# A gated mix of attention and feed-forward: the first head's query tile filled on chip, and new prices in VectorE's budget

## The chip, the core and the metric

One core of a Trainium2 chip runs one program. The time is the device time of an execution in microseconds. Engines: TensorE (PE; its weight loads are shown as PEld), VectorE (DVE), ScalarE (ACT), GpSimd (POOL), and SyncE (SP), which issues nearly all DMAs, in order.

## The reference

```python
q = (x @ wq) in 32 heads of 16;  k = x @ wk;  v = x @ wv      # one k and v for all heads
a = concat_h(softmax(q_h @ k.T * 16**-0.5) @ v) @ wo
b = (silu(x @ w_gate) * (x @ w_up)) @ w_down
g = sigmoid((x * gate_w).sum(-1))
out = g * a + (1 - g) * b       # x: 2048 x 512, w_gate: 512 x 1792, all float32
```

## The kernel before

The 2048 rows of x are four chunks `c` of 512. Products that need float32 accuracy are made of three matmuls of a high and a low part (names ending in h and l). The 512 query columns are four groups `m` of 8 heads; `query(m, c)` (L229) is one job of 12 matmuls into a PSUM tile `pf`, of which there are three.

When a query job is done, its `keep` (L242) makes three 128x512 tiles from `pf`: the high part, the low part, and a bound on the scores. For early jobs ScalarE does the high part and the bound (L257, L258) and VectorE the low part (L259) and a maximum (`most`, L276). Each tile's 16 rows per head then go to the DRAM tensor `q_d` (L265), four stores of 256 KB per job, one of them the high part again. A head `h` is later read back as one tile `qs` of 512 KB, from `q_d[h]` (L672 for head 0, L688 for the others).

**Opening.** x is transposed, k and v are projected, then the four jobs `query(0, c)` run, then (1,2), (1,3) and (2,3) in `fill(GAP)` (L675). Between them SP gets the stores, the load of the fourth query weight (L671), the load of head 0's `qs` (L672) and the loads of the first gate and up weight (L144). A loaded weight lies in one of two buffers `wraw` until POOL has split it into two parts (L111, L112).

**Main part.** 128 blocks follow, four per head. A block (L749) makes eight score tiles (L698, two matmuls each, into two PSUM buffers `pss`), for which ScalarE takes the exponential (L706), part of it from a copy by VectorE (L702). Between the scores, in an order written out in STEPS, stand 16 steps of other matmuls (L198): query jobs that are left, gate, up and down projections. Each of these jobs is done in two halves of 64 rows, and the second half follows a marker, a tiny memset on VectorE (L446). At the end stand the products of exponentials and values (L718), whose sum over a head is divided on VectorE (L727, L730).

**VectorE's budget.** Work that may wait is put in a list, DEFER, with a price: the gate's multiply after the tanh (`silu`, L321, 0.7), the cast of gate times up in two parts (L111, L112, 1.2), and for late query jobs `scale` (L269), `bound` (L272, and then the store of the bound) and `most` (L276). At the end of a block, BUDGET = 3.8 is what may be done (L781 to L797): first items of the division, then three passes over DEFER: items of gates from earlier blocks, items of a gate whose tanh was in this block (in the set FRESH), and query items. What does not fit stays. If a gate's multiply is still in the list when its up projection is done, the up step does it itself, just ahead of its own product (L330, L331).

## Time and profile before

| | us |
|---|---|
| median of 3 runs | 1348.66 |
| lowest, highest | 1347.03, 1348.97 |
| the profiled execution | 1348.94 |
| its span, first to last instruction | 1347.0 |
| PE, ACT, DVE, POOL busy in the span | 1328.4, 1076.9, 722.0, 221.4 |

A row of the timeline is: start, duration, engine, line, operation, written tile <- read tiles, shapes, count; in brackets the idle time of the engine ahead of it and what ended that. A row of waits is: who <- whom, total, times, longest. Rows with SPq are DMA issues.

### The profile page before, as it was taken

What the parts mean: (1) busy time and instruction counts of PE and PEld (TensorE: products, weight loads), DVE (VectorE), ACT (ScalarE), POOL (GpSimd) and SP (SyncE); (2) the same over time, 40 slices, a digit from 0 to 9 for tenths busy, and PEclk for the clock granted to TensorE, in tenths of its full rate; (3) what the DMA queues carried; (4) which work ended last, traced back from release to release, by engine and by line L of the source; (5) the groups of instructions that cost most, each with busy time, mean ns of one, the idle gap of its engine ahead of it and who ended that gap; (6) DMA issues with size and microseconds to landing.
All of it is one profiled execution on the core that took longest, in us unless ns stands there. A gap on an engine that the chain in (4) does not pass through costs nothing. (4 is left out here: it accounts for less than half of the span.)

```text
span 1347.0 us, 26709 instructions
## 1 busy us (share of the span) xinstructions
PE 1328.4 (99%) x10743; PEld 767.6 (57%) x10743; DVE 722.0 (54%) x1237; ACT 1076.9 (80%) x1508; POOL 221.4 (16%) x227
## 2 busy tenths in 40 slices
PE   9899999999999999999999999999999999999998
PEld 7655555555555555555555555555555555555586
DVE  5346664654655664565465565456455565455442
ACT  4488898888888888888888888888888888888511
POOL 6352211420321430232110000000000000001222
PEclk9799999999999999999999999999999999999999
DMA  8851211411351751462262442243132342233164
GB/s 279 275 160 41 75 37 43 122 44 36 102 190 58 257 155 35 153 208 83 68 198 104 123 152 83 68 129 96 40 114 64 118 156 68 99 107 114 40 196 143
DMA packets 101041, 156.03 MB, mean 116 GB/s; under 512 B 11568, under 2 KB 42544, under 8 KB 99248
## 3 DMA queue, kind: packets, MB, share of 16 engines
q1 hardware_dynamic: 99184, 154.05, 35.9%
q8 instruction: 88, 1.44, 0.5%
q10 hardware_dynamic: 1728, 0.20, 0.1%
q14 instruction: 41, 0.34, 0.1%
HBM read 98.63 MB, written 55.57 MB: 114 GB/s over the span
## 5 line engine op out<-in xcount | busy, mean ns | idle before, releaser
L706 ACT ACTIVATE pt<-pss 128x1024 f32<-128x1024 f32 (+1 forms) x1024 | 833.0, 864 | 172.8 <-PE pss L698 146.4
L702 DVE COPY pt<-pss 128x512 f32<-128x512 f32 x381 | 263.5, 692 | 449.9 <-PE pss L698 413.8
L718 PE MATMUL po<-pt,vaug 128*32 128x512 f32 x4096 | 466.0, 595 | 0.0
L698 PE MATMUL pss<-qs,ks 64*128 64x512 f32 x2048 | 400.4, 416 | 6.7 <-DMA qs<-q_d 4.5
L698 PEld LDWEIGHTS pss<-qs,ks 64*128 64x128 f32 x2048 | 192.0, 185 | 219.5 <-ACT pt L706 172.3
L718 PEld LDWEIGHTS po<-pt,vaug 128*32 128x32 f32 x4096 | 120.0, 109 | 263.5 <-issue 257.8
L706 ACT ACTIVATE pt<-pt 128x512 f32<-128x512 f32 x381 | 210.5, 620 | 0.0
L198 PE MATMUL pf<-xh,wgh 64*128 64x512 f32 (+1 forms) x440 | 163.3, 392 | 2.2 <-DVE sign L446 1.8
L198 PE MATMUL pf<-xh,wgl 64*128 64x512 f32 (+1 forms) x440 | 162.7, 391 | 0.0
L198 PE MATMUL pf<-xl,wgh 64*128 64x512 f32 (+1 forms) x440 | 162.6, 391 | 0.0
L198 PE MATMUL pf<-xh,wuh 64*128 64x512 f32 (+1 forms) x440 | 161.0, 392 | 0.1
L198 PE MATMUL pf<-xh,wul 64*128 64x512 f32 (+1 forms) x440 | 160.2, 392 | 0.0
L198 PE MATMUL pf<-xl,wuh 64*128 64x512 f32 (+1 forms) x440 | 159.5, 390 | 0.0
L198 PE MATMUL pf<-wdh,hl 64*128 64x512 f32 (+1 forms) x427 | 143.5, 390 | 0.0
L198 PE MATMUL pf<-wdh,hh 64*128 64x512 f32 (+1 forms) x427 | 143.1, 392 | 0.0
L198 PE MATMUL pf<-wdl,hh 64*128 64x512 f32 (+1 forms) x427 | 142.8, 390 | 0.0
L727 DVE RECIPROCAL rsb<-rsb 128x128 f32<-128x128 f32 x128 | 117.0, 935 | 7.1 <-issue 4.5
L474 POOL CAST xh<-wraw 128x512 fp32r<-128x512 f32 x4 | 2.4, 611 | 548.2 <-DMA wraw<-o_d 548.2
L198 PEld LDWEIGHTS pf<-xh,wgh 64*128 64x128 f32 (+1 forms) x440 | 79.5, 185 | 12.5 <-issue 3.3
L198 PEld LDWEIGHTS pf<-xh,wuh 64*128 64x128 f32 (+1 forms) x440 | 78.7, 185 | 9.9 <-issue 1.7
L198 PEld LDWEIGHTS pf<-xl,wgh 64*128 64x128 f32 (+1 forms) x440 | 79.8, 185 | 5.7
L198 PEld LDWEIGHTS pf<-xh,wgl 64*128 64x128 f32 (+1 forms) x440 | 79.8, 185 | 5.6
(136 smaller groups left out, 1368.0 us busy)
## 6 DMA issues: line engine op xcount, KB each, us to landing
qs<-q_d SPq DMA_DIRECT2D x32, 512.0 KB, 4.9
wraw<-in_B_w_gate_dram SPq DMA_DIRECT2D x28, 256.0 KB, 3.5
wraw<-in_B_w_up_dram SPq DMA_DIRECT2D x28, 256.0 KB, 3.7
wraw<-in_B_w_down_dram SPq DMA_DIRECT2D x28, 256.0 KB, 4.0
wgh<-w_d SPq DMA_DIRECT2D x28, 256.0 KB, 2.8
wgl<-w_d SPq DMA_DIRECT2D x28, 256.0 KB, 3.0
wuh<-w_d SPq DMA_DIRECT2D x28, 256.0 KB, 2.7
wul<-w_d SPq DMA_DIRECT2D x28, 256.0 KB, 2.9
```

Source lines behind the costliest of these rows:

```text
L198: ins = nc.tensor.matmul(self.ps, a, b, start=(i == 0 and not half), stop=(last and half != 0))
L474: nc.gpsimd.tensor_copy(OT[c][0][:, k, :], raw)
L698: nc.tensor.matmul(ps[:, b * CH:(b + 1) * CH], ks[rows, kt * P:(kt + 1) * P], QS[h][rows, j, :], start=True, stop=True)
L702: other = nc.vector.tensor_copy(pt[:, CH:], ps[:, CH:]) if half else None
L706: ins = nc.scalar.activation(pt[:, w], ps[:, w], AF.Exp, scale=SCALE)
L718: nc.tensor.matmul(po[c * 2 * DH:(c + 1) * 2 * DH, :], vaug[:, kt, :], pt[:, c * CH:(c + 1) * CH], start=(kt == 0), stop=(kt == NT - 1))
L727: nc.vector.reciprocal(rsb[:, w], rsb[:, w])
```

## The change

Three edits.

1. Head 0's `qs` is no longer read back from `q_d`. The tile is made ahead of the queries, and each `query(0, c)` fills its part of it with four DMAs of 32 KB from its own cast tiles: 16 of their 128 rows, every eighth one. The stores of these jobs to `q_d` are collected in STORES and issued behind the last of the jobs, still ahead of the load of the fourth query weight.
2. The prices of late query work rise: `scale` 0.5 to 1.0, `bound` 0.7 to 1.8.
3. In the first pass over DEFER, room is kept for multiplies (price under 1) of gates whose tanh was in this block.

```diff
-    WQ, QS = {}, {}
+    WQ, QS, STORES = {}, {}, []
...
             parts = [ql, qh, qb.bitcast(F32R)]
+            if not m:
+                for h, qs in QS.items():
+                    for i, j in enumerate((1, 0, 1, 2)):
+                        row = c % 2 * RT + i * DH
+                        nc.sync.dma_start(qs[row:row + DH, c // 2, :].bitcast(F32),
+                                          parts[j].bitcast(F32).rearrange("(r h) s -> h r s", h=HG)[h])
...
-                (SOON if late else DEFER).extend([((m, c), 0.5, scale), ((m, c), 0.7, bound), ((m, c), 0.7, most)])
+                (SOON if late else DEFER).extend([((m, c), 1.0, scale), ((m, c), 1.8, bound), ((m, c), 0.7, most)])
             else:
-                store()
+                if m:
+                    store()
+                else:
+                    STORES.append(store)
                 most()
...
             load_x(3, 2)
+            new_qs(0)
             project_kv(0)
...
+            run(STORES, NCH)
             load_wq(3)
-            nc.sync.dma_start(new_qs(0).bitcast(F32), q_d[0])
...
                     n, cost, f = item
-                    if n in kept or (2 if isinstance(n, tuple) else n in FRESH) != stage or cost > left:
+                    keep = sum(d[1] for d in DEFER if d[0] in FRESH and d[1] < 1) if not stage else 0
+                    if n in kept or (2 if isinstance(n, tuple) else n in FRESH) != stage or cost > left - keep:
```

The order of instructions moves in three places. First SP behind the queries 0, before (the last two stores of their sixteen, then the loads, then the stores of (1,2)):

```order
L265 DMA q_d<-hh 16x8x512
L265 DMA q_d<-hl 16x8x512
L225 DMA wraw<-in_A_wq_dram 128x4x128
L672 DMA qs<-q_d 128x1024
L144 DMA wraw<-in_B_w_gate_dram 128x4x128
L144 DMA wraw<-in_B_w_up_dram 128x4x128
L265 DMA q_d<-hh 16x8x512
L265 DMA q_d<-hl 16x8x512
```

and now, from the last copies of chunk 3 on (the line numbers of the change are up to 12 higher: L265 is the copy, L272 the store, L699 the load of head 1, which was L688):

```order
L265 DMA qs<-hh 16x512
L265 DMA qs<-hl 16x512
L272 DMA q_d<-hh 16x8x512
L272 DMA q_d<-hl 16x8x512
L272 DMA q_d<-hh 16x8x512 x3
...
L225 DMA wraw<-in_A_wq_dram 128x4x128
L144 DMA wraw<-in_B_w_gate_dram 128x4x128
L699 DMA qs<-q_d 128x1024
L144 DMA wraw<-in_B_w_up_dram 128x4x128
L272 DMA q_d<-hh 16x8x512
```

All sixteen stores of queries 0 stand behind all sixteen copies, and the load of head 1, which waits for these stores, has moved ahead of the up weight and of the twelve stores of the jobs (1,2), (1,3) and (2,3).

ScalarE at the start of the main part, before (high part and bound of (1,2), (1,3), (2,3), then exponentials):

```order
L257 ACTIVATE hh<-pf 128x512
L258 ACTIVATE ht<-pf,kmax 128x512
L257 ACTIVATE hh<-pf 128x512
L258 ACTIVATE hs<-pf,kmax 128x512
L257 ACTIVATE hh<-pf 128x512
L258 ACTIVATE ht<-pf,kmax 128x512
L706 ACTIVATE pt<-pss 128x1024 x5
```

and now (L717 is the exponential):

```order
L257 ACTIVATE hh<-pf 128x512
L258 ACTIVATE ht<-pf,kmax 128x512
L717 ACTIVATE pt<-pss 128x1024
L257 ACTIVATE hh<-pf 128x512
L258 ACTIVATE hs<-pf,kmax 128x512
L257 ACTIVATE hh<-pf 128x512
L258 ACTIVATE ht<-pf,kmax 128x512
L717 ACTIVATE pt<-pss 128x1024 x4
```

The first exponential has moved ahead of the evacuations of (1,3) and (2,3).

VectorE from the end of block 21 to the marker in block 22, before (L727 the division, L111 and L112 a cast, L702 the copies of scores, L321 the gate's multiply, L331 the product with up):

```order
L303 COPY hs<-pf 128x512
L727 RECIPROCAL rsb<-rsb 128x128 x2
L111 CAST hh<-ht 128x512
L112 TENSOR_TENSOR hl<-ht,hh 128x512
L702 COPY pt<-pss 128x512
L446 MEMSET sign 1x1
L702 COPY pt<-pss 128x512 x2
L321 SCALAR_TENSOR_TENSOR ht<-ht,hs 128x512
L331 TENSOR_TENSOR ht<-ht,pf 128x512
L446 MEMSET sign 1x1
```

and now (L331 is the gate's multiply here, L341 the product):

```order
L313 COPY hs<-pf 128x512
L738 RECIPROCAL rsb<-rsb 128x128 x2
L331 SCALAR_TENSOR_TENSOR ht<-ht,hs 128x512
L713 COPY pt<-pss 128x512
L456 MEMSET sign 1x1
L713 COPY pt<-pss 128x512 x2
L341 TENSOR_TENSOR ht<-ht,pf 128x512
L456 MEMSET sign 1x1
```

The multiply has moved to the end of block 21, and the cast that stood there to the end of block 22. In the same way the bounds of late query jobs move to later blocks (the first from block 7 to block 14, the fourth from block 42 to block 47), and block 36 takes a gate job ahead of the down jobs, whose cast is now a block later.

## The prediction

> **What bounds the kernel now.** I read the page's totals and clock row first, then TensorE's waits, then the time by stretches.

> ```profile
> PE 1328.4 (99%) x10743; PEld 767.6 (57%) x10743; DVE 722.0 (54%) x1237; ACT 1076.9 (80%) x1508; POOL 221.4 (16%) x227
> ...
> PEclk9799999999999999999999999999999999999999
> ```

> TensorE (PE) is busy almost throughout, so only three things can make it end earlier: an idle gap, a low clock, or work taken off it. No matmul is removed. The clock row has one dent, in the second slice of 34 us. Its gaps:

> ```profile
> PE pss L698 <- DMA qs<-q_d: 4.5, 1, 4.5
> PE pf L198 <- DVE sign L446: 1.8, 2, 1.6
> PE pss L698 <- DVE sign L446: 1.6, 1, 1.6
> ```

> One wait of 4.5 us is for the first head's query tile, coming back from DRAM. Two of 1.6 us are for VectorE's marker between the halves of a projection. By stretches (us, busy time of PE, PEld, DVE, ACT, POOL, then clock):

> ```profile
> 52.97:66.63 13.66, 13.39 (x49) 10.04 (x48) 2.13 (x4) 8.53 (x10) 3.77 (x4) 0.50 0.93 286
> ...
> 266.22:277.50 11.28, 9.69 (x83) 5.23 (x81) 7.60 (x14) 9.63 (x16) 2.65 (x3) 1.00 0.08 23
> 466.25:477.44 11.19, 9.61 (x83) 5.33 (x81) 8.91 (x13) 8.57 (x14) 4.48 (x4) 1.00 0.68 217
> 287.04:296.40 9.36, 9.36 (x82) 5.13 (x81) 4.85 (x10) 8.46 (x14) 3.08 (x4) 1.00 0.52 155
> ```

> The last row is an ordinary block, 9.36 us with PE full. The two above it hold the VectorE waits and cost 1.92 and 1.83 more. The first row is the dent: 13.66 us at half clock, right after the 4.5 us gap. So the change's places are worth at most 4.5, some 6.8 (half of 13.66) and 3.75 us.

> **The start, step by step.**

> ```profile
> 47.76 0.39 PE L198 MATMUL pf<-xh,acc 128*128 128x512 f32 x1
> 52.67 0.56 PE L698 MATMUL pss<-qs,ks 64*128 64x512 f32 x2 [4.52 <-DMA qs<-q_d]
> ```
> ```profile
> 67.76 3.64 PE L718 MATMUL po<-pt,vaug 128*32 128x512 f32 x32
> ```

> PE ends the early queries at 48.15, scores at 52.67, and first multiplies by the values (L718) at 67.76. *When is the tile there now?* The last part of chunk 3 is cast on VectorE; a 32 KB DMA of 16 rows and a 256 KB store give the prices of a copy:

> ```profile
> 41.24 0.69 DVE L259 TENSOR_TENSOR hl<-pf,hh 128x512 fp32r<-128x512 f32 x1 [1.44 <-ACT hl L258]
> ```
> ```profile
> 133.68 1.75 SPq L732 DMA_DIRECT2D o_d<-osb  x4
> ```
> ```profile
> q_d<-hh SPq DMA_DIRECT2D x20, 256.0 KB, 3.8
> o_d<-osb SPq DMA_DIRECT2D x128, 32.0 KB, 1.7
> ```

> Three copies go out from 41.93 on, 0.44 each (1.75/4), so the last leaves by 43.3 and lands at 45.0, at 47.1 were it as slow as a store: before 48.15 either way. A copy between two on-chip tiles is not in the trace; I take 1.7, the row of its size. The sixteen issues cost SP 7 us, in which it otherwise waits for casts. [...] So the **4.52 us go**.

> What is late next is ScalarE. Its new order puts the first exponential ahead of the evacuations of queries (1,3) and (2,3), which had all come before it:

> ```profile
> 48.24 0.60 ACT L257 ACTIVATE hh<-pf 128x512 fp32r<-128x512 f32 x1 [1.54 <-issue]
> 48.73 0.68 ACT L258 ACTIVATE ht<-pf,kmax 128x512 fp32r<-128x512 f32 x1
> 53.26 1.94 ACT L706 ACTIVATE pt<-pss 128x1024 f32<-128x1024 f32 x2 [3.85 <-PE pss L698]
> ```

> The first exponential starts 0.6 after the first score (53.26 against 52.67), at 48.75, and ends at 49.75. Two evacuations follow, 1.17 each (48.24 to 49.41), to 52.1; exponentials 2 to 4, 0.95 each, end at 53.05, 54.0 and 54.9. With two score buffers, score 4 waits from about 50.7 for exponential 2, a **new hole of 2.35 us**, and scores 5 and 6 for 3 and 4. After score 6 the block has 22 steps. A step is (9.36 - 3.64)/24 = 0.24 us, 3.64 being a block's value products; so 54.9 + 5.3 + 0.4 for the turn gives the first L718 at 60.6 against 67.76, a **gain of 7.2**. Bounds: without ScalarE's delay 36 steps from 48.15 end at 57.2 (gain 10.6); at half clock from 53 on the gain shrinks to 2.4.

> *The clock.* Here a gap of 4.52 us was followed by 13.66 us at 0.50; a gap of 2.35 is not in the trace. [...]

> *The weights.* The sixteen stores of queries 0 now go out only after the last copy, ahead of the fourth query weight and the gate weights:

> ```profile
> 52.95 0.55 SPq L265 DMA_DIRECT2D q_d<-hh  x1
> ...
> 61.80 0.57 SPq L265 DMA_DIRECT2D q_d<-ht  x1
> ```
> ```profile
> 49.87 1.04 POOL L111 CAST acc<-wraw 128x512 fp32r<-128x512 f32 x1 [11.46 <-DMA wraw<-in_A_wq_dram]
> 50.99 1.51 POOL L112 TENSOR_TENSOR acc<-wraw,acc 128x512 fp32r<-128x512 f32 x1
> ...
> 69.14 0.61 POOL L111 CAST wgh<-wraw 128x512 fp32r<-128x512 f32 x1 [11.70 <-DMA wraw<-in_B_w_gate_dram]
> ...
> 90.90 0.61 POOL L111 CAST wgh<-wraw 128x512 fp32r<-128x512 f32 x1 [5.57 <-DMA wraw<-in_B_w_gate_dram]
> ```
> ```profile
> 71.89 0.39 PE L198 MATMUL pf<-xh,wgh 64*128 64x512 f32 x1
> ```
> ```profile
> 100.84 0.39 PE L198 MATMUL pf<-xh,wgh 64*128 64x512 f32 x2
> ```

> Twelve such stores took 0.80 each (52.95 to 61.80), so sixteen from 43.3 end near 55.3, landed 59.1; the query weight lands behind them at 59.9 and is split till 62.5, the gate's first weight till 64.4. PE wants it 4.1 after the first L718 (71.89 - 67.76), at 64.7: just in time. The twelve next stores wait behind the up weight, whose buffer the split frees at 62.5; they end, landed, near 75.9 (12 x 0.80 + 3.8), and gate weight 1 behind them near 76.5. The split of weight 2 came 21.8 after that of weight 1 (90.90 - 69.14), through five down weights and then eight stores on SP; four of the eight now go out ahead of or between the down weights, so I take 4 x 0.80 off: 18.5, a split at 95.0, half done at 95.6. PE wants it 33.1 after the first L718 (100.84 - 67.76), at 93.7. **Cost 1.9 us**, between 0 and 4. Such delays don't add up: a late weight moves PE, and its later needs with it.

> **VectorE's budget.** Block 22, from 266.22, and block 43, from 466.25:

> ```profile
> 274.11 1.39 DVE L321 SCALAR_TENSOR_TENSOR ht<-ht,hs 128x512 f32<-128x512 f32 x1
> ...
> 275.53 0.69 DVE L331 TENSOR_TENSOR ht<-ht,pf 128x512 f32<-128x512 f32 x1
> ...
> 276.37 0.46 PE L198 MATMUL pf<-xh,wgh 64*128 64x512 f32 x1 [1.59 <-DVE sign L446]
> ```
> ```profile
> 466.28 0.94 DVE L727 RECIPROCAL rsb<-rsb 128x128 f32<-128x128 f32 x1
> 467.88 1.00 DVE L335 SCALAR_TENSOR_TENSOR ht<-hs,ht 128x512 f32<-128x512 f32 x1 [0.66 <-ACT hs L317]
> 468.92 1.39 DVE L111 CAST hh<-ht 128x512 fp32r<-128x512 f32 x1
> 470.34 0.98 DVE L112 TENSOR_TENSOR hl<-ht,hh 128x512 fp32r<-128x512 f32 x1
> 471.25 1.78 DVE L272 SCALAR_TENSOR_TENSOR qh<-qh 128x512 fp32r<-128x512 f32 x1
> ...
> 473.56 0.06 DVE L446 MEMSET sign<- 1x1 f32 x1
> ...
> 473.77 0.50 PE L698 MATMUL pss<-qs,ks 64*128 64x512 f32 x2 [1.58 <-DVE sign L446]
> ```

> In the first the gate's multiply (L321) was left over from the block before and runs just ahead of the up product that needs it; the marker waits behind both. The new order has it at the end of the block before, in place of a cast. In the second the bound (L272, 1.78 us, priced 0.7) closes a tail of 6.1 us (the five rows from 466.28) and the marker comes late; priced at 1.8 it goes to a lighter block. Counting every block's tail with measured durations, none of the new order exceeds 4.0 us, and tails of 4.5 in the old order made no wait. So **both excesses go, 3.75 us**; I count 3.65. Bounds: 1.8 (one stays) and 5 (the smaller excesses, 0.2 to 0.4 in some blocks, go too).

> **Sum.** 1347.0 - 7.2 + 1.9 - 3.65 = 1338.05 for the span; the profiled execution took 1.94 more than its span (1348.94), so **1340.0**. That execution lies 0.3 above the median of the runs, 1348.66.

> **Rivals.**
> - *The clock falls again* at the 2.35 us hole and its followers: the gain at the start is 2.4, weights are then in time: 1347.0 - 2.4 - 3.65 + 1.94 = 1342.9. For it: PE is idle for 3.5 of the 6.8 us from 48.15. Against: no single gap nears 4.52. 10%.
> - *Weights come later*, 3 to 6 us instead of 1.9: 1341 to 1344. For it: SP is one queue, and the load of head 1's tile waits there for all sixteen stores. 13%.
> - *The pricing does not do what it says*: a moved cast or bound makes a new wait as large as the old: 1343. 8%.
> - *Slower*: ScalarE is in order. The evacuation of (1,3) reuses the first chunk's cast tile, which is free only when that chunk's third store has landed: issued 44.9, landed 48.7, wanted at 49.75. Every exponential stands behind it. From 1 us of lateness on, each us costs one; it eats the whole gain of 9.0 only if the store lands near 59, 14 us after its issue against the 3.8 of the row. Then 1349 to 1353. 5%, with some of it in "same".
> - *Better*: ScalarE's delay is hidden or the weights are in time: 1334 to 1337. 9%.

> The forecast keeps 55%, 1338 to 1342. To hold eight in ten, the range takes in the better case and the first three rivals but for their ends: 1334.5 to 1344.5. A measurement here tells about 0.2% (2.7 us) from no change: faster 0.90, within 0.05, slower 0.05.

> **What would show it.** No wait for qs before the first score, and that score at 48; clock 1.00 in 50 to 67; a hole of about 2.3 us ahead of the fourth score, ended by ScalarE; the first L718 near 60.6; a wait of PE for POOL's wgh between 64 and 96, some 2 us in all; no wait for the marker near blocks 22 and 43. I am wrong if the first score still waits, if the clock dips, or if new marker waits stand elsewhere.

## The result, and the profile after

The changed kernel took **1348.12 us** in the median of 14 runs (1344.35 to 1350.62), the kernel before 1348.26 (14 runs, 1345.89 to 1351.83): a ratio of 0.9996, interval 0.9985 to 1.0006. No difference can be measured; the forecast was 1340.0, and its range ended at 1344.5. The profiled execution of the changed kernel took 1346.55, with a span of 1344.5.

Lines of the changed kernel are some ten further down: the scores are L709, the exponentials L717, the products with the values L729, the marker L456, the copies into `qs` L265 and the stores L272. First TensorE's busy time and the clock's row, then its waits inside the main part (us in total, times, longest):

```profile
PE 1327.6 (99%) x10743; PEld 765.3 (57%) x10743; DVE 720.7 (54%) x1237; ACT 1075.8 (80%) x1508; POOL 220.4 (16%) x227
...
PEclk9899999999999999999999999999999999999999
```
```profile
PE pss L709 <- ACT pt L717: 2.2, 3, 1.8
PE pf L198 <- POOL wgh L111: 1.6, 1, 1.6
...
PE pf L198 <- POOL wgl L112: 0.6, 1, 0.6
PE pss L709 <- DVE sign L456: 0.6, 1, 0.6
PE pf L198 <- DVE sign L456: 0.6, 2, 0.4
```

The 4.5 us wait for `qs` is gone, and so are both 1.6 us waits for the marker. The longest wait for ScalarE was 0.3 us before and is 1.8 now, and the waits for POOL's gate weight are new. The clock's row still has a dent in its second slice. The waits in time, PE's first and then ScalarE's:

```profile
51.00 0.62 PE L198 MATMUL pf<-xh,acc 64*128 64x512 f32 x2
53.47 0.50 PE L709 MATMUL pss<-qs,ks 64*128 64x512 f32 x2 [1.85 <-ACT pt L717]
53.81 0.39 PE L198 MATMUL pf<-xl,acc 64*128 64x512 f32 x1
54.39 1.71 PE L709 MATMUL pss<-qs,ks 64*128 64x512 f32 x4 [0.19 <-ACT pt L717]
```
```profile
49.35 1.02 ACT L717 ACTIVATE pt<-pss 128x1024 f32<-128x1024 f32 x1 [4.77 <-issue]
50.27 0.59 ACT L257 ACTIVATE hh<-pf 128x512 fp32r<-128x512 f32 x1
...
51.80 0.71 ACT L258 ACTIVATE ht<-pf,kmax 128x512 fp32r<-128x512 f32 x1
```

The hole before the fourth score is there, as forecast, 1.85 us. The granted clock in stretches of 3.41 us, counted from where it changes (us, busy time and number for PE, PEld, DVE, ACT, POOL, then the clock):

```profile
47.56:50.97 3.41, 3.38 (x17) 2.23 (x16) 0.00 (x0) 1.62 (x3) 0.00 (x0) 1.00 0.97 314
50.97:54.38 3.41, 1.38 (x6) 0.48 (x4) 2.47 (x4) 3.41 (x6) 0.00 (x0) 1.00 0.96 324
54.39:57.79 3.40, 3.28 (x11) 2.28 (x12) 0.69 (x1) 2.35 (x3) 0.00 (x0) 0.50 1.00 333
57.80:61.20 3.40, 3.40 (x14) 2.70 (x15) 0.75 (x2) 1.62 (x2) 0.00 (x0) 0.50 0.98 294
61.22:64.62 3.40, 3.40 (x30) 1.99 (x32) 0.75 (x2) 3.21 (x6) 3.20 (x4) 1.00 0.53 167
```

So the clock fell behind the hole, and stayed at half for two stretches of 3.41 us, against four in the kernel before. Then the third gate weight: SyncE's issues of weights, POOL's split, and PE's wait:

```profile
74.50 0.54 SPq L144 DMA_DIRECT2D wraw<-in_B_w_gate_dram  x1
...
86.21 5.16 SPq L144 DMA_DIRECT2D wraw<-in_B_w_down_dram  x3
...
93.41 0.54 SPq L144 DMA_DIRECT2D wraw<-in_B_w_gate_dram  x1
```
```profile
98.84 0.61 POOL L111 CAST wgh<-wraw 128x512 fp32r<-128x512 f32 x1 [2.61 <-DMA wraw<-in_B_w_gate_dram]
```
```profile
99.50 0.50 PE L198 MATMUL pf<-xh,wgh 64*128 64x512 f32 x2 [1.60 <-POOL wgh L111]
```

Blocks 22 and 43, which had taken 11.28 and 11.19:

```profile
266.17:275.90 9.73, 9.63 (x82) 5.13 (x80) 5.84 (x11) 8.79 (x14) 2.62 (x3) 1.00 0.09 27
464.81:474.18 9.37, 9.37 (x82) 5.29 (x80) 7.07 (x12) 8.45 (x14) 5.56 (x6) 1.00 0.71 234
```

For all kernels of this study, the profiled execution can be cut at three places: the first product with the values (the end of the opening), that of the fifth block, and the last block's. The times are starts of those matmuls in PE's timeline.

| kernel | median us | ratio to before, 95% | first | fifth block | last | span |
|---|---|---|---|---|---|---|
| before | 1348.26 | | 67.76 | 106.11 | 1267.20 | 1347.0 |
| changed | 1348.12 | 0.9985 to 1.0006 | 63.52 | 105.78 | 1264.34 | 1344.5 |
| e1 prices alone | 1345.06 | 0.9971 to 0.9989 | 67.12 | 105.46 | 1263.04 | 1342.2 |
| e2 copies alone | 1347.67 | 0.9988 to 1.0006 | 64.93 | 105.92 | 1267.33 | 1347.0 |
| e3 free buffers | 1342.81 | 0.9948 to 0.9975 | 61.35 | 103.72 | 1261.34 | 1340.6 |
| e4 two weights first | 1341.88 | 0.9938 to 0.9965 | 61.36 | 105.73 | 1263.37 | 1342.9 |
| e5 before, rows filled | 1344.78 | 0.9960 to 0.9984 | 64.59 | 103.36 | 1263.63 | 1343.0 |
| e6 changed, rows filled | 1347.47 | 0.9986 to 1.0004 | 61.21 | 104.01 | 1263.32 | 1343.3 |
| e7 = e3 and e4 | 1342.30 | 0.9938 to 0.9965 | 62.19 | 104.84 | 1263.69 | 1343.4 |
| e8 = e7, rows filled | 1346.43 | 0.9977 to 0.9995 | 58.30 | 102.42 | 1262.01 | 1342.2 |
| e9 = e3, all weights early | 1337.29 | 0.9905 to 0.9932 | 59.28 | 98.39 | 1256.34 | 1335.7 |
| e10 = e9, rows filled | 1339.93 | 0.9924 to 0.9952 | 58.31 | 97.62 | 1256.07 | 1335.5 |
| e11 changed, again | 1348.03 | 0.9988 to 1.0006 | 63.44 | 108.10 | 1266.80 | 1346.8 |
| e12 all weights early alone | 1342.62 | 0.9944 to 0.9971 | 64.73 | 103.11 | 1261.98 | 1341.2 |

The ratio is to runs of the kernel before on the same chip (medians 1347.8 to 1348.6). A profiled execution may lie off its kernel's median: those of e4 and e7 were the longest of their five.

### The profile page after: what moved, and what is told of

Same layout as the page of the kernel before. It is cut to its first block, busy times and chain, and to the rows that moved or that the text cites. A ratio compares the mean times of both kernels' runs of the same rounds, so it can differ in the third digit from the quotient of the medians.

```text
span 1344.5 us, 26729 instructions
## 1 busy us (share of the span) xinstructions
PE 1327.6 (99%) x10743; PEld 765.3 (57%) x10743; DVE 720.7 (54%) x1237; ACT 1075.8 (80%) x1508; POOL 220.4 (16%) x227
## 3 DMA queue, kind: packets, MB, share of 16 engines
q8 instruction: 88, 1.44, 0.5%
## 5 line engine op out<-in xcount | busy, mean ns | idle before, releaser
L717 ACT ACTIVATE pt<-pss 128x1024 f32<-128x1024 f32 (+1 forms) x1024 | 832.4, 864 | 173.5 <-PE pss L709 142.2
L729 PE MATMUL po<-pt,vaug 128*32 128x512 f32 x4096 | 466.0, 595 | 0.0
L709 PE MATMUL pss<-qs,ks 64*128 64x512 f32 x2048 | 397.0, 415 | 3.6 <-ACT pt L717 2.2
L709 PEld LDWEIGHTS pss<-qs,ks 64*128 64x128 f32 x2048 | 190.1, 184 | 217.7 <-ACT pt L717 177.0
L729 PEld LDWEIGHTS po<-pt,vaug 128*32 128x32 f32 x4096 | 120.0, 109 | 263.2 <-issue 257.6
L717 ACT ACTIVATE pt<-pt 128x512 f32<-128x512 f32 x381 | 210.6, 620 | 0.0
L198 PE MATMUL pf<-xh,wgh 64*128 64x512 f32 (+1 forms) x440 | 163.2, 393 | 2.7 <-POOL wgh L111 1.6
L198 PE MATMUL pf<-xh,wgl 64*128 64x512 f32 (+1 forms) x440 | 162.8, 392 | 0.6 <-POOL wgl L112 0.6
L198 PE MATMUL pf<-xl,wgh 64*128 64x512 f32 (+1 forms) x440 | 162.6, 391 | 0.0
L198 PE MATMUL pf<-xh,wuh 64*128 64x512 f32 (+1 forms) x440 | 161.1, 392 | 0.1
L198 PE MATMUL pf<-xh,wul 64*128 64x512 f32 (+1 forms) x440 | 160.4, 392 | 0.0
L198 PE MATMUL pf<-xl,wuh 64*128 64x512 f32 (+1 forms) x440 | 159.5, 390 | 0.0
L198 PE MATMUL pf<-wdh,hl 64*128 64x512 f32 (+1 forms) x427 | 143.5, 390 | 0.0
L198 PE MATMUL pf<-wdh,hh 64*128 64x512 f32 (+1 forms) x427 | 143.3, 392 | 0.0
L198 PE MATMUL pf<-wdl,hh 64*128 64x512 f32 (+1 forms) x427 | 143.2, 390 | 0.0
L198 PEld LDWEIGHTS pf<-xh,wgh 64*128 64x128 f32 (+1 forms) x440 | 79.5, 185 | 13.5 <-POOL wgh L111 2.4
L198 PEld LDWEIGHTS pf<-xh,wuh 64*128 64x128 f32 (+1 forms) x440 | 78.8, 185 | 9.2 <-issue 1.5
L198 PEld LDWEIGHTS pf<-xh,wgl 64*128 64x128 f32 (+1 forms) x440 | 79.8, 185 | 7.1 <-POOL wgl L112 1.2
L198 PEld LDWEIGHTS pf<-xl,wgh 64*128 64x128 f32 (+1 forms) x440 | 79.8, 185 | 6.1
## 6 DMA issues: line engine op xcount, KB each, us to landing
wraw<-in_B_w_gate_dram SPq DMA_DIRECT2D x28, 256.0 KB, 3.4
wraw<-in_B_w_up_dram SPq DMA_DIRECT2D x28, 256.0 KB, 3.6
wraw<-in_B_w_down_dram SPq DMA_DIRECT2D x28, 256.0 KB, 4.1
wgh<-w_d SPq DMA_DIRECT2D x28, 256.0 KB, 2.7
wgl<-w_d SPq DMA_DIRECT2D x28, 256.0 KB, 2.9
wuh<-w_d SPq DMA_DIRECT2D x28, 256.0 KB, 2.7
wul<-w_d SPq DMA_DIRECT2D x28, 256.0 KB, 2.9
```

Source lines behind the costliest of these rows:

```text
L198: ins = nc.tensor.matmul(self.ps, a, b, start=(i == 0 and not half), stop=(last and half != 0))
L709: nc.tensor.matmul(ps[:, b * CH:(b + 1) * CH], ks[rows, kt * P:(kt + 1) * P], QS[h][rows, j, :], start=True, stop=True)
L717: ins = nc.scalar.activation(pt[:, w], ps[:, w], AF.Exp, scale=SCALE)
L729: nc.tensor.matmul(po[c * 2 * DH:(c + 1) * 2 * DH, :], vaug[:, kt, :], pt[:, c * CH:(c + 1) * CH], start=(kt == 0), stop=(kt == NT - 1))
```

## The experiments

**The two parts by themselves.** e1 is the kernel before with the prices and the kept room, e2 the changed kernel without them.

```diff
-                (SOON if late else DEFER).extend([((m, c), 0.5, scale), ((m, c), 0.7, bound), ((m, c), 0.7, most)])
+                (SOON if late else DEFER).extend([((m, c), 1.0, scale), ((m, c), 1.8, bound), ((m, c), 0.7, most)])
...
+                    keep = sum(d[1] for d in DEFER if d[0] in FRESH and d[1] < 1) if not stage else 0
-                    if n in kept or (2 if isinstance(n, tuple) else n in FRESH) != stage or cost > left:
+                    if n in kept or (2 if isinstance(n, tuple) else n in FRESH) != stage or cost > left - keep:
```

> The kernel before with the new prices and the room kept for the gate's multiply, and without the copies. My theory (the copies' gain is eaten at the start, the price part earns what was forecast): the marker waits of blocks 22 and 43 go, some 3.4 us, so 1344.9 against 1348.3, ratio 0.9975. Rival (the prices move the waits to other blocks: in the changed kernel blocks 11, 32, 53 and 118 are 0.34 to 0.36 longer each): 3.4 - 1.4 = 2.0 us, 1346.3, ratio 0.9985. If the prices do nothing: 1348.3. The clock dips as before (0.993 to 0.994 listed), the wait for qs stays at 4.5 us.

Measured: 1345.06, 2.9 less than before, between the two theories and nearer the first. In the trace the stretch from the fifth block to the last shrank from 1161.08 (1267.20 - 106.11, before rounding) to 1157.59, by 3.5: block 22 takes 9.74 and block 43 9.38. Blocks 11 and 32 are not longer here, so those 0.35 us of the changed kernel are no price of the pricing by itself.

> The changed kernel with the old prices and no kept room: the copies alone. My theory: in most executions the clock dip after the new hole is as long as it was before, and the late weights cost some 3.9 us in blocks 1 to 4, so the copies by themselves are worth -0.4 (the profiled execution: 4.24 earlier at the first value product, 3.88 given back) to +3 us: 1348 to 1351, ratio 1.000 to 1.0025. Rival (the copies gain the 4.5 us of the wait and the prices lose it): 1344, ratio 0.997. A hole of 1.85 us before the fourth score and a clock of 0.5 behind it.

Measured: 1347.67, no difference from before, and 0.3 below the expected range. The wait for `qs` is gone, the hole of 1.85 is there, and the low clock lasted a third stretch, with PE busy throughout:

```profile
50.75:54.15 3.40, 1.51 (x8) 0.59 (x5) 2.47 (x4) 3.40 (x7) 0.00 (x0) 1.00 1.04 344
54.16:57.56 3.40, 3.15 (x11) 2.16 (x12) 0.69 (x1) 2.48 (x4) 0.00 (x0) 0.50 0.99 334
57.57:60.97 3.40, 3.40 (x15) 2.73 (x15) 0.75 (x2) 1.62 (x2) 0.00 (x0) 0.50 0.98 290
60.98:64.39 3.41, 3.41 (x19) 2.65 (x16) 0.69 (x1) 2.54 (x4) 2.63 (x3) 0.50 0.61 184
```

The first value product came at 64.93 instead of 63.52, the fifth block at the same time, 105.92. So the copies alone earn nothing, and something makes the fifth block start near 106 wherever the first began.

**Two mends of the opening.** ScalarE's new order came with the held-back stores: the evacuations of (1,3) and (2,3) need the first chunk's cast tiles, so the scheduler put the first exponential ahead of them. e3 gives these two jobs the down weights' buffers, which POOL first writes at 84.21 us in the changed kernel; ScalarE's order is then as before. e4 loads two weights ahead of the stores. e7 has both.

```diff
+                spare = (m, c) in EARLY_Q[1:]
-                qh = wp.tile([P, CH], F32R, name="hh", bufs=7)
+                qh = wp.tile([P, CH], F32R, name="wdh" if spare else "hh", bufs=5 if spare else 7)
```
```diff
+            load_wq(3)
+            load_w("g", 0)
             run(STORES, NCH)
-            load_wq(3)
-            for nm in "gu":
-                load_w(nm, 0)
+            load_w("u", 0)
```

> The changed kernel, with the cast tiles of queries (1,3) and (2,3) in two buffers that lie free then (those of the down weights), so that they wait for no store. ScalarE's order is then again evacuations first, exponentials after. My theory (a hole that ScalarE's order makes starts the clock dip): no hole before the fourth score, clock 1.00 from 48 to 70 in every execution, first value product at 57 to 59 instead of 63.5; the weights are then later against the need, so PE waits 2 to 5 us for the gate's first and third weight; 1343 to 1346, and the runs lie closer together than the 6 us of the changed kernel. Rival (the clock falls anyway, or the late weights set the pace alone): 1347 to 1349.

Measured: 1342.81, runs within 1.3 us of each other. The time is 0.2 below the expected range, but not for the expected reason: there is no hole of more than 0.6 us, and the clock fell all the same, so the first value product came at 61.35 and not at 57 to 59.

```profile
49.12:52.52 3.40, 2.57 (x12) 1.18 (x10) 1.28 (x2) 3.40 (x5) 0.00 (x0) 1.00 1.01 322
52.54:55.94 3.40, 3.09 (x10) 2.46 (x11) 0.75 (x2) 1.73 (x3) 0.00 (x0) 0.50 1.01 343
55.95:59.35 3.40, 3.40 (x14) 2.72 (x14) 1.21 (x2) 2.18 (x3) 0.00 (x0) 0.50 1.02 316
```

In the stretch ahead of the dip PE was idle for 0.83 of 3.40 us. My theory that the hole starts the dip does not hold here.

> The changed kernel with the fourth query weight and the gate's first weight issued ahead of the sixteen held-back stores (the up weight behind them). My theory (the late weights cost 2.2 us of waits for POOL and more behind): PE's waits for POOL's wgh and wgl between 64 and 110 go, 2 to 3.5 us: 1344.6 to 1346. Rival (the weights are behind the twelve next stores as well, or the time goes elsewhere): 1347.5 to 1348.5, waits for POOL as before. [...]

Measured: 1341.88, better than expected in the median. Its trace is of the longest of the five executions (1344.85) and shows a wait of 2.8 us for the third gate weight, and behind it a second dip, of two stretches, in block 4.

```profile
PE pf L198 <- POOL wgh L111: 2.8, 1, 2.8
```
```profile
93.14:96.54 3.40, 1.50 (x12) 0.30 (x4) 0.69 (x1) 1.59 (x3) 0.28 (x1) 1.00 0.85 255
96.56:99.96 3.40, 2.38 (x10) 1.48 (x12) 0.00 (x0) 0.00 (x0) 3.02 (x4) 0.50 0.04 10
99.97:103.37 3.40, 3.40 (x20) 2.65 (x18) 1.29 (x2) 1.62 (x2) 1.83 (x3) 0.50 0.88 296
```

> The changed kernel with both mends: the cast tiles of (1,3) and (2,3) in free buffers, and the fourth query weight and the gate's first weight ahead of the held-back stores. My theory: the small waits for ScalarE remain (0.6 us each) and the dip is one or two stretches, as in each mend alone; waits for the first gate weight go, the third gate weight is still late; first value product at 59 to 61, 1339.5 to 1342. Rival (the two mends earn the same time, since what comes earlier waits for the third gate weight): 1341.5 to 1343.

Measured: 1342.30. The rival held: both mends earn what one does. The trace has the opening's dip of two stretches (53.93 to 60.73), the wait for the third gate weight (1.8 us) and a dip of one stretch behind that.

**The rows in use and the clock.** A job's steps use 64 of the array's 128 rows (64*128 in the traces, against 128*128 of the queries in the opening). Two jobs run side by side on all of them (in the changed kernel, steps that start at 92.57 and 92.59), but in the opening the first is alone. e5, e6 and e8 add, beside each of the lone steps (expected to be 18, 17 in the traces), the same step of the other 64 rows, into a tile that nobody reads:

```diff
                 job.step(i, 0)
+                if not self.high and self.steps <= PADS:
...
+                    a, b = job.terms[i]
+                    nc.tensor.matmul(PAD[0], a[RT:], b[RT:], start=True, stop=True)
```

> The kernel before, with 18 matmuls added whose result nobody reads: beside each of the first steps that use only rows 0 to 63 of TensorE's array, the same step of rows 64 to 127 into a spare tile. No other engine's order changes. My theory (the clock looks at how much of the array worked in stretches of 3.41 us, and the 13.65 us dip lasts because the first steps use half the rows): the 4.5 us wait still starts a dip at the end of its stretch, but it lasts one or two stretches, 3.4 or 6.8 us, instead of four, and the time falls by 3.4 to 5.1 us from 1348 to 1343 to 1344.6. Rival (only idle time counts, or the dip's length is fixed): dip of 13.65, 1348; and if the added matmuls cost time of their own, up to 18 x 0.21 = 3.8 us more.

Measured: 1344.78, 3.6 less than before and 0.2 above the range; the dip lasts two stretches, of which the first lies mostly in the wait for `qs`:

```profile
47.29:50.69 3.40, 1.43 (x7) 0.85 (x5) 1.96 (x4) 1.18 (x2) 0.30 (x1) 1.00 0.80 211
50.71:54.11 3.40, 1.03 (x6) 0.92 (x8) 0.59 (x1) 0.20 (x1) 2.53 (x3) 0.50 0.62 218
54.12:57.52 3.40, 3.40 (x20) 2.87 (x17) 0.00 (x0) 2.76 (x3) 3.04 (x4) 0.50 0.90 280
57.54:60.94 3.40, 2.75 (x24) 2.17 (x22) 0.75 (x2) 2.43 (x3) 0.42 (x1) 1.00 0.96 313
```

The stretch from 54.12 brought the clock back, with 20 matmuls. In the kernel before, after the same wait, PE was as busy, with fewer matmuls, and the clock came back only behind the last of these rows:

```profile
59.80:63.21 3.41, 3.41 (x12) 2.71 (x13) 1.05 (x3) 1.18 (x3) 0.00 (x0) 0.50 1.00 318
63.22:66.63 3.41, 3.41 (x18) 2.62 (x18) 0.69 (x1) 2.04 (x3) 0.00 (x0) 0.50 1.00 286
```

PE's idle time, which is none in these three stretches, and a fixed length do not explain that: the dip lasted 6.81 us here (50.71 to 57.52) and 13.65 there. The number of matmuls goes along with it: the clock came back behind 20 here and behind 18 there, and stayed at half behind 12.

> The changed kernel with the same added matmuls. The hole before the fourth score stays, since ScalarE makes it. My theory: the clock still falls behind the hole, but for one stretch of 3.41 us in place of two to four, so the runs lie closer together and near the fast end of the changed kernel's, 1343 to 1345.5 against 1348.1. Rival (idle time alone): dips of two to four stretches, 1348.

In the profiled execution (1345.30, inside the range) the dip is one stretch, as expected, the first value product is at 61.21, and the fourth block has its wait for the gate weight (1.6 us). The median is 1347.47 all the same, 2 us above the range, and the runs spread over 4 us. Each run has its mean granted clock on record: 0.998 in this execution and the one as fast, 0.995 in the four longest (1348.69 to 1349.34). A difference of 0.003 over 1347 us is some 8 us more at half clock, which is some 4 us of time (an estimate from these figures) and as much as the spread. So the longer executions had further dips; where they lay, no trace shows.

> Both mends and the added matmuls. My theory: with PE's waits under 1 us and the other half of the array in use no stretch falls below the clock's bound, so no dip between 45 and 70: the first value product near 58, 1.7 to 3.4 us earlier than without the added matmuls; of that the third gate weight gives part back, 1338 to 1341. Rival (the dip comes from idle time and stays): the same as without them, within 0.7 us.

The opening has no dip, with PE idle for 0.76 us in the first of these stretches:

```profile
48.83:52.24 3.41, 2.65 (x20) 1.32 (x16) 1.28 (x2) 3.41 (x5) 3.03 (x3) 1.00 0.99 323
52.24:55.65 3.41, 3.00 (x28) 2.31 (x27) 1.44 (x3) 2.84 (x5) 0.00 (x0) 1.00 0.99 330
```

The first value product is the earliest of all, 58.30, and the median is 1346.43, far outside the expectation and 4.1 above e7. In the trace PE reaches the second gate weight 2.9 us too early, and a dip follows from 79.55 to 82.96:

```profile
PE pf L199 <- POOL wgh L112: 2.9, 1, 2.9
```

That does not explain the medians: the traced executions took 1344.39 here and 1345.44 in e7, and what the longer executions of e8 did is open. Against e3 (idle 0.83, 12 matmuls, dip) this is the cleanest pair on the clock: idle time alike (0.76), 20 matmuls, no dip.

**The weights.** e9 takes e3, issues the fourth query weight and the first gate weight ahead of the sixteen held-back stores and the first up, second gate and second up weight among them, and puts the five down weights in the list that is taken up after the first jobs:

```diff
-            run(STORES, NCH)
             load_wq(3)
-            for nm in "gu":
-                load_w(nm, 0)
+            load_w("g", 0)
+            for nm, n in (("u", 0), ("g", 1), ("u", 1)):
+                run(STORES, 1)
+                load_w(nm, n)
+            run(STORES, 1)
...
-        for nm in "gu":
-            load_w(nm, 1)
-        for n in GROUPS[0]:
-            load_w("d", n)
+        LOADS.extend([lambda n=n: load_w("d", n) for n in GROUPS[0]])
```

e10 adds the matmuls of e8, e11 is the changed kernel once more, e12 is e9 without the free buffers.

> The changed kernel with the cast tiles of (1,3) and (2,3) in free buffers, and all early weights ahead: the fourth query weight, then the first and second gate and up weights among the sixteen held-back stores, and the five down weights taken up after the first jobs in place of ahead of the third gate weight. My theory (whatever the start gains is taken back at the fourth block's end by the third gate weight; in all runs so far the fifth block's value products begin at 102.4 to 106.1, though the first ones lie between 58.3 and 67.8): no waits for POOL over 0.5 us, the first four blocks take 38.4 to 39 us as before, so first value product 61 to 62, the fifth block's at 100, 1339 to 1341. Rival (something else sets block 4, or the third gate weight is still late behind the stores of (1,0) and (1,1)): 1342 to 1344, fifth block at 103 to 105.

Measured: **1337.29**, 10.5 us less than before (ratio 0.9918, interval 0.9905 to 0.9932), all five runs within 1.6 us. That is 1.7 below the expected 1339 to 1341. There is no dip before the last matmul, and the granted clock of the five runs is 0.999 to 1.000. The third gate weight is split 8.0 us earlier than in the changed kernel, and PE waits for no weight:

```profile
90.83 0.61 POOL L111 CAST wgh<-wraw 128x512 fp32r<-128x512 f32 x1 [1.22 <-DMA wraw<-in_B_w_gate_dram]
```
```profile
47.46:50.87 3.41, 2.90 (x14) 1.79 (x12) 1.98 (x4) 2.05 (x4) 2.76 (x3) 1.00 1.01 304
50.87:54.28 3.41, 2.74 (x13) 1.64 (x14) 0.44 (x2) 3.41 (x5) 1.68 (x2) 1.00 0.80 260
54.29:57.69 3.40, 3.40 (x23) 2.73 (x23) 2.04 (x4) 2.77 (x5) 1.90 (x2) 1.00 0.96 285
```

The first four blocks take 39.1 us (98.39 - 59.28), 38.4 in the kernel before. Several loads moved at once, so which of them earns what is not shown.

> The same with the 18 added matmuls on the unused rows. My theory: no dip (first value product at 58.3 as with both mends and the added matmuls), and now nothing takes it back: the fifth block's at 96.7 to 97.5, 1336 to 1338. Rival (a start that early finds the weights late whatever their order, as with both mends and the added matmuls at 1346.4): 1341 to 1346, with waits for POOL of 2 us and more and a dip behind them.

The trace is as expected within 0.1 us, 58.31 and 97.62, but the median is 1339.93, 2.6 above e9. Four of five runs took at least 2 us more than the profiled one, at a granted clock of 0.999 against its 1.000, and no trace shows what they did; that stays open.

> The changed kernel once more, for a second trace and for a comparison on one chip with the two above. My theory: 1347.5 to 1348.5; the dip lasts two to four stretches of 3.41 us from one execution to the next, the first value product lies at 63.5 to 67, and the fifth block's at 105.8 within 0.5 all the same, since the third gate weight sets it. Rival (the dip's length goes through to the end): the fifth block's comes later by what the dip is longer, 109.

Measured: 1348.03. The second trace has the same hole, the same dip of two stretches and the same first value product (63.44), but not the same fifth block: 108.10. The wait for the third gate weight is 2.9 us here, and has a dip of its own behind it.

```profile
PE pf L198 <- POOL wgh L111: 2.9, 1, 2.9
```
```profile
98.62:102.02 3.40, 1.06 (x6) 0.59 (x8) 0.00 (x0) 0.11 (x1) 2.27 (x3) 1.00 0.39 116
102.04:105.44 3.40, 3.40 (x20) 2.66 (x17) 1.29 (x2) 1.62 (x2) 2.04 (x3) 0.50 0.70 247
```

My expectation of 105.8 within 0.5 missed it: the weight sets when block 4 goes on, and a dip behind the wait puts another 1.7 us (half of 3.41) on top. Besides the length of the wait, its place may count, by an estimate of where the stretches end. In the first trace the clock changes at 61.21 and next at 1341.21, 1280.00 us later, which is 375 steps of 3.413; counted on in such steps from 61.21, a stretch ends at 98.76, inside the wait of 1.6 us from 97.90 to 99.50, which brought no dip. Counted on in the same way from 60.73 in e7, the wait of 1.8, from 95.45 to 97.23, lies inside one stretch (94.9 to 98.3) and brought one.

> The changed kernel with all early weights ahead, as in the run that took 1337.3, but without the free buffers: ScalarE has three exponentials ahead of the evacuations of (1,3) and (2,3) again, as in the run with only two weights ahead. My theory (two separate costs: the hole with the dip that it starts, and the third gate weight): the hole of 2.5 us and a dip of one or two stretches of 3.41 us stay, first value product at 61.4 to 63.5, but the first four blocks take 38.4 to 39 us, so the fifth block's at 100 to 102.3 and 1339.5 to 1342. Rival (the weights were all of it, the hole is hidden): 1337 to 1338; or (the hole was all of it): 1346 and more.

Measured: 1342.62, 0.6 above the range. The hole and its dip are there, and the first four blocks take 38.4. The first value product, 64.73, is later than expected, since this execution has a dip of one stretch much earlier, while k and v are projected (the first row of the second fence): from the first of those matmuls to the first query it takes 16.66 us, 15.41 in the changed kernel.

```profile
PE pss L711 <- ACT pt L719: 2.9, 3, 2.5
```
```profile
11.66:15.07 3.41, 3.41 (x12) 2.77 (x11) 3.02 (x4) 1.02 (x1) 1.93 (x2) 0.50 0.67 215
...
52.63:56.03 3.40, 0.79 (x5) 0.19 (x2) 1.28 (x2) 3.40 (x7) 2.29 (x3) 1.00 0.88 262
56.05:59.45 3.40, 3.31 (x11) 2.68 (x12) 1.94 (x4) 1.51 (x3) 0.55 (x1) 0.50 0.95 295
```

With e9 this makes a square (the medians are of different chips, on which the kernel before took 1347.8 to 1348.6): changed kernel 1348.0, free buffers 1342.8 (-5.2), all weights early 1342.6 (-5.4), both 1337.3 (-10.7). The two costs are separate and add up. With only two weights ahead they do not: e4 alone takes 1341.9, and with the free buffers (e7) 1342.3, where PE still waits 1.8 us for the third gate weight and a dip follows.

## Why the prediction was wrong

It named the right mechanisms and expected most of their directions. Two steps of the sum failed, and the rivals that stood for them were each priced as if the other did not occur. By the terms, for the two traces of the changed kernel:

| term | forecast | first trace | second trace |
|---|---|---|---|
| opening, to the first value product | -7.2 | -4.24 | -4.32 |
| first four blocks (forecast: late weights) | +1.9 | +3.92 | +6.31 |
| fifth block to the last (VectorE) | -3.65 | -2.53 | -2.38 |
| end, and outside the span | 0 | +0.47 | +0.27 |
| sum, to 1348.94 (terms rounded) | 1340.0 | 1346.55 | 1348.82 |

- **The copies in time**: right. The first score starts at 48.74, without a wait; a copy's issue cost 0.54 to 0.58 instead of 0.44 and landed after 1.9 in the median instead of 1.7, which changed nothing.
- **The hole**: right in place and cause, 1.85 instead of 2.35.
- **The full clock**: this step failed. The forecast had one gap to go by: behind 4.52 the clock had been low, and 2.35 was not in the trace. That the clock stays full behind 2.35, which the gain of 7.2 takes for granted, no run shows; behind the 1.85 of the changed kernel the dip came, 6.83 us long, which costs 3.4; the first value product was 2.9 later than forecast (63.52 against 60.6), since the smaller hole gave 0.5 back. That "no single gap nears 4.52" was no argument: in e3 the clock fell without any gap over 0.6.
- **"Cost 1.9 us" of the weights**: the other step that failed, by 2.0 us in one trace and 4.4 in the other. Of the 3.92 of the first trace, 2.77 lie in the block with the wait for the third gate weight. The forecast had nothing for the rest: 0.85 in the block before it, where PE waits 0.59 for VectorE's marker, and 0.31 in the first. Of the 6.31 of the second, 5.58 lie in the block with that wait and its dip. The third gate weight was forecast to be split at 95.0 and was at 98.84 and, in the second trace, 99.67: gate weight 1 was already 2.6 late (79.09 against 76.5) and the distance between the two 19.75 against 18.5. PE's need was forecast at 93.7 and came at 97.9, since the dip had delayed PE too. That late weights could make a dip of their own was not considered.
- **VectorE's budget**: right in its mechanism, 1.1 too large in size. Both excesses went (1.55 and 1.82 us), and e1 earns 3.5 in its trace. In the changed kernel blocks 11, 32, 53 and 118 are 0.34 to 0.36 longer each, which the term left out; PE waits there for nothing that the profile shows. The traces of e1 to e4, e9 and e10 lack this in blocks 11 and 32. What brings it is open.
- **The slower rival** did not come: the evacuation of (1,3) starts at 50.27, right behind the first exponential, with no wait for a store.

The two failing terms are most of what the change lost: the forecast without the weights' 1.9 is 1338.1, and e9, where the granted clock is 0.999 to 1.000 and no weight is late, took 1337.3. (That the two lie so near is partly luck, since e9 has no hole either, and the forecast had one.) So the gain was there, and was given back in the opening's dip and at the third gate weight. That the copies earn nothing (e2), the prices 2.9 (e1), and both together 0.1, is not explained to the last us: the second dip of e11 is what I can show for it. How much low clock the runs without a trace had can be read from their granted clocks: 0.993 to 0.996 in the 25 runs of the changed kernel, with a median of 0.994, which is also the median of the kernel before. The first trace, at 0.996, was among the highest; it has 10.1 us at half clock, the few at the end included, and at 0.994 it is some 16 (twice 0.006 of 1346, an estimate). So in the median execution the clock stays low about as long as before the change. Where the further dips lie, only the second trace shows.

## What to carry to other kernels

When a transfer is moved out of the way, follow the queue it is moved into to the end: the copies freed the first score at 48.7, and the stores they held back cost nearly the same time 50 us later (4.24 gained and 3.92 given back in the first trace), most of it at a weight that stood behind them. A late weight on the engine that sets the pace can cost more than its wait: in the second trace of the changed kernel PE waited 2.9 us, and then ran 3.41 us at half clock. Two rivals that can occur together want a case of their own, with a chance.

## What the runs showed of the hardware

```profile
46.15:49.56 3.41, 2.00 (x9) 1.31 (x7) 1.40 (x3) 1.72 (x3) 0.00 (x0) 1.00 0.83 249
```

PE is busy for 2.00 us there, less than e3's 2.57. That the rows in use are what differs is my estimate from these counts and from the added matmuls. With those, the opening's dip lasted two stretches in e5 against four in the kernel before, one in e6 against two in the changed kernel, and none in e8 against two in e7. What the clock goes by was not shown, and no bound was tested.
